# Side work of an attention, expert and feed-forward kernel put in other places

## The chip, the cores and the metric

The kernel runs on one core of one Trainium2 chip. The core has a matrix engine (TensorE, PE in the profile, with its weight loads as PEld), a vector engine (VectorE, DVE), a scalar engine (ScalarE, ACT), GpSimd (POOL) and a sequencer that only issues DMAs here (SyncE, SP). Each engine works through its own instructions in order and waits on semaphores for the others. The metric is the device time of one execution in microseconds (us), less is better, given as the median of the runs.

## The reference

```python
def reference(**kwargs):
    attn_out = _attn_ref(q, k, v, cap)          # (4, 12, 448, 64)
    x = attn_out.transpose(0, 2, 1, 3).reshape(1792, 768)
    x = _moe_ref(x, ...)                        # 8 experts, 768 -> 1024 -> 768
    return _moe2_ref(x, ...)                    # 768 -> 1536 -> 768

def _attn_ref(q, k, v, cap):
    scores = cap * np.tanh(q @ k.T / 8 / cap)
    attn = np.exp(scores - scores.max(-1)); attn /= attn.sum(-1) + 1e-09
    return attn @ v

def _moe_ref(x, modality_id, w_gate, modality_bias, w1, w2):
    logits = x @ w_gate + modality_bias[modality_id]
    e_idx = np.argmax(logits, axis=1); gate_w = softmax(logits)[e_idx]
    for e in range(E):
        mask = e_idx == e
        out[mask] = gate_w[mask, None] * (np.maximum(x[mask] @ w1[e], 0.0) @ w2[e])

def _moe2_ref(x, w_gate, w_val, w_out):
    return (sigmoid(x @ w_gate) * (x @ w_val)) @ w_out
```

The output is float32 throughout.

## The kernel before, in words

All matrix products are made on PE in f16. A float32 operand is split in two f16 parts: "hi", the operand itself rounded, and "lo", the operand less hi. Nearly every split is one ACT instruction for hi and one DVE (or GpSimd) instruction for lo that reads what ACT wrote, so the two engines pass work back and forth.

The kernel is written under a manual schedule: the order in which the Python code issues instructions is the order on each engine, and nothing reorders them.

**Attention** goes over 4 batches and 12 heads; a step makes exponentials of scores on ACT (L300, L305), products on PE (L314, L316) and sums of exponentials on DVE (L325, L327, L333); L318 copies a finished head pair out of PSUM. The table `AFTER` (L66) lists for each batch after which step side work is issued. Its entry for the third batch holds the start of the experts: `w1` loads of the first expert's first weights, `w1s` their split (`split_w` L676: six pieces of 128x1024, hi L687, lo L689), `gather` the fetching of tokens into `xg` (L695, an indirect DMA that GpSimd issues), `trx` (L710) the transposes of those tokens on PE (L705) with their hi on ACT (L707) and lo on DVE (L708) into `xT`, and `w2` the loads of the second weights. `M["trs"]` lists the PSUM banks that transposes take in turn (L248); at this point it is one bank.

**Experts.** Tokens are sorted by expert into blocks of 128 rows; 15 blocks have work with this input, 14 of them always (`NFULL`). `step(s, fill)` (L764) is a block, run one behind: the products with w1 of block s (`mm1`, 36 matmuls of 512 columns), relu, w1's split for the next block if its expert is new, transposes of block s+2, then `fill[0]`, the DMAs that are due, the first half of block s-1's products with w2 (`mm2`, 24 matmuls of 384 columns), the transposes of block s's hidden values (`trh`), the second half, the output `put_y` (ACT L753, DVE L754, indirect DMA L755) and `fill[1]`. The fills hold work for the feed-forward: its weights arrive as 64-bit floats and are converted by three integer DVE operations and an ACT scale (`conv_ops` L836 to L847), two conversions a block; weight sums `wo_job`; and `y_sums` (L950).

**Feed-forward.** It uses Winograd's scheme with seven products and needs sums of blocks of its left operand. `y_sums(sup, p)` makes them for 128 rows p: four stages a, b, d, e, each of two or three DVE operations, a hi on ACT (L905) and a lo on DVE (L902); `y_more` (L1348) does the same under a condition on the number of blocks. The tokens go through in two groups (sup 0 with 512 columns, sup 1 with 384). In sup 1 the sums stand among weight sums (L883, L905, L910) and the copies and additions of sup 0's last products (ACT L1112, DVE L1115). `rest` (L1339) runs the blocks beyond 14 as they exist; behind it the passage (L1404 to L1420) begins the feed-forward's products (L1019) and does the last block's `mm2`.

Of the kernel before, what the change touches and what calls it, by code (L numbers as in the profile page):

```python
# [69 lines left out]
def tile_kernel(ctx: ExitStack, tc: tile.TileContext, q, k, v, cap, mod, wg, mb, w1, w2, gw, vw, ow, out, dbg=None):  # L70
# [1545 lines left out]
```

## Time and profile before

| | us |
|---|---|
| median of 3 runs (lowest, highest) | 1010.03 (1008.42, 1010.03) |
| the profiled execution's own time | 1006.74 |
| its span in the trace | 1004.8 |
| PE busy | 927.0 (92%) |
| DVE busy | 716.5 (71%) |
| ACT busy | 503.0 (50%) |
| GpSimd busy | 178.2 (18%) |

The profiled execution's mean granted TensorE clock is 0.978 of full. All rows are from that one execution. Attention lies at 0 to about 254 us, the experts at 254 to about 540, the feed-forward behind. In a row of a timeline the bracket tells how long the engine had been idle and which instruction released it; a letter q behind an engine's name is its sequencer (branches, register loads).

### The profile page before, as it was taken

Reading aid. Unit: us, or ns where it says so; the run is one execution under the profiler, and the core shown is the slowest. Engines: PE = TensorE matmul, PEld = TensorE weight load, DVE = VectorE, ACT = ScalarE, POOL = GpSimd, SP = SyncE. Lnnn points to the kernel's source line nnn. Section 1 sums busy time; section 2 is a strip of 40 time slices with the busy share of each in tenths; the row PEclk is TensorE's granted clock in tenths of the full one; section 3 lists DMA queues with packets and bytes.
Section 4 is the critical chain, followed back from the end, with each engine's and each line's share of the span. In section 5 each row is a group of like instructions: output and inputs, shape, how many; then the busy total and the mean of one; then the engine's idle time right before and its main releaser. Section 6 shows DMA issues by size and latency. Waiting matters only on the chain. (4 is left out here: it accounts for less than half of the span.)

```text
span 1004.8 us, 14723 instructions
## 1 busy us (share of the span) xinstructions
PE 927.0 (92%) x5291; PEld 474.4 (47%) x5291; DVE 716.5 (71%) x1239; ACT 503.0 (50%) x814; POOL 178.2 (18%) x219
## 2 busy tenths in 40 slices
PE   6998989876999899999996999999989899999997
PEld 2333333332455445555454444444556456666554
DVE  4879889689584896468773899997698754545651
ACT  5978769665414463334451665544344345554320
POOL 3000000001012131111120000000000078883131
PEclk9999999998899999999998999999999999999999
DMA  5534464446235678767930464321062132220001
GB/s 126 156 109 117 113 186 120 123 135 230 80 105 189 222 252 273 224 200 256 299 103 29 113 234 165 111 95 63 17 99 106 48 110 80 68 75 1 1 32 64
DMA packets 120491, 128.78 MB, mean 128 GB/s; under 512 B 75232, under 2 KB 100720, under 8 KB 119632
## 3 DMA queue, kind: packets, MB, share of 16 engines
q1 hardware_dynamic: 116288, 108.22, 35.6%
q0 software_dynamic: 4112, 19.46, 5.8%
q8 instruction: 44, 0.72, 0.3%
q14 instruction: 47, 0.39, 0.1%
HBM read 91.16 MB, written 30.99 MB: 122 GB/s over the span
## 5 line engine op out<-in xcount | busy, mean ns | idle before, releaser
L745 PE MATMUL sc<-w2s,hs 128*128 128x384 f16 x720 | 126.3, 331 | 13.3 <-ACTq L767 4.3
L1019 PEld LDWEIGHTS <-wa 128*128 128x128 f16 x909 | 89.8, 99 | 90.0 <-issue 11.6
L726 PE MATMUL sc<-w1s,xT 128*128 128x512 f16 x540 | 121.4, 383 | 0.9 <-DVE xT L708 0.7
L1019 PE MATMUL pp<-yr,wa 128*128 128x512 f16 (+1 forms) x468 | 101.7, 373 | 9.5 <-DVEq L1341 7.9
L745 PEld LDWEIGHTS <-hs 128*128 128x128 f16 x720 | 71.1, 99 | 57.9 <-issue 12.1
L300 ACT ACTIVATE E<-sc,sct 128x896 f32<-128x896 f32 x72 | 72.4, 1006 | 44.6 <-PE sc L292 43.5
L726 PEld LDWEIGHTS <-xT 128*128 128x128 f16 x540 | 53.2, 99 | 64.8 <-issue 3.2
L1019 PE MATMUL pp<-zr,wa 128*128 128x384 f16 x441 | 75.8, 326 | 0.6 <-ACT yr L1067 0.6
L305 ACT ACTIVATE E<-E,capt 128x896 f32<-128x896 f32 x72 | 74.7, 1038 | 0.6
L883 DVE TENSOR_TENSOR sta<-sta 128x384 f32<-128x384 f32 x108 | 71.0, 696 | 3.5 <-POOL y L910 2.5
L1019 PE MATMUL pp<-wos,yr 128*128 128x384 f16 x378 | 63.7, 331 | 8.0 <-ACT hs L1112 8.0
L314 PE MATMUL ot<-E,vf 128*64 128x448 f32 x288 | 70.4, 570 | 0.0
L1101 POOL DMA_INDIRECT out_dram<-hs,pm x14 | 14.0, 998 | 273.1 <-DVE hs L1115 198.9
L292 PE MATMUL sc<-qT,kT 64*128 64x448 f16 x432 | 56.2, 368 | 0.8 <-DVE kT L259 0.8
L1019 PEld LDWEIGHTS <-yr 128*128 128x128 f16 x378 | 37.5, 99 | 34.2 <-issue 10.6
L1019 PEld LDWEIGHTS <-wb 128*128 128x128 f16 x378 | 37.0, 98 | 34.5
L905 ACT ACTIVATE wa<-sta 128x384 f16<-128x384 f32 x98 | 48.6, 513 | 7.2 <-DVE sta L883 4.2
L1049 DVE TENSOR_TENSOR yr<-yr,pp 128x384 f32<-128x384 f32 x24 | 13.2, 552 | 43.1 <-PE pp L1019 43.1
L1019 PE MATMUL pp<-yr,wb 128*128 128x512 f16 x189 | 43.9, 379 | 0.0
L999 PE MATMUL pp<-wos,sta 128*128 128x384 f16 x252 | 41.9, 326 | 0.0
L708 DVE TENSOR_TENSOR xT<-tr,xT 128x384 f16<-128x384 f32 x34 | 17.4, 552 | 33.8 <-ACT xT L707 31.8
L910 POOL TENSOR_TENSOR wa<-sta,wa 128x384 f16<-128x384 f32 x42 | 40.1, 972 | 4.1 <-ACT wa L905 4.1
(308 smaller groups left out, 1598.6 us busy)
## 6 DMA issues: line engine op xcount, KB each, us to landing
sta<-g SPq DMA_DIRECT2D x40, 384.0 KB, 3.1
st<-in_moe_w_dram SPq DMA_DIRECT2D x8, 1536.0 KB, 10.2
sta<-in_moe_w_out_dram SPq DMA_DIRECT2D x12, 768.0 KB, 4.4
sta<-in_moe_w_val_dram SPq DMA_DIRECT2D x12, 768.0 KB, 6.3
g<-sta SPq DMA_DIRECT2D x18, 384.0 KB, 3.0
qf<-in_q_dram SPq DMA_DIRECT2D x48, 112.0 KB, 3.3
kf<-in_k_dram SPq DMA_DIRECT2D x48, 96.0 KB, 2.8
vf<-in_v_dram SPq DMA_DIRECT2D x24, 192.0 KB, 3.1
```

Source lines behind the costliest of these rows:

```text
L292: nc.tensor.matmul(sc[:, h, :S], kt_[p, a, 128 * j:128 * j + 128], qt_[p, b_], start=i == 0, stop=i == 2)
L300: nc.scalar.activation(out=e, in_=src, func=AF.Tanh, scale=sct)
L305: nc.scalar.activation(out=e, in_=e, func=AF.Exp, scale=capt)
L314: nc.tensor.matmul(ot[g][64 * h:64 * h + 64, :S], vf[g][:, h, j], e[:, h], start=j == 0, stop=False)
L708: nc.vector.tensor_tensor(out=lo, in0=pt[:, :128 * n], in1=hi, op=ALU.subtract)
L726: nc.tensor.matmul(p[:, nh], xT[s % 2][:, a, kk], w1s[:, b_, kk, 512 * nh:512 * nh + 512], start=i == 0, stop=i == 17)
L745: nc.tensor.matmul(M["p2"][:, nh, :384], hT[par][:, a, kk], w2s[:, b_, kk, 384 * nh:384 * nh + 384], start=i == 0, stop=i == 23)
L883: tt = lambda eng, o, x, y, op: eng.tensor_tensor(out=o, in0=x, in1=y, op=op)
L905: nc.scalar.activation(out=hi, in_=src, func=AF.Copy)
L910: los = [lambda x=x, d=d, e=e: e.tensor_tensor(out=d[1], in0=x, in1=d[0], op=ALU.subtract) for x, d, e in todo]
L999: nc.tensor.matmul(bk[p][:, c0:c1], l(p, a, kk), r(p, b_, kk)[:, c0:c1], start=i == 0, stop=i == 3 * kn - 1)
L1019: nc.tensor.matmul(bk[c][:, c0:c1], l(p, a, kk), r(p, b_, kk)[:, c0:c1], start=i == c0 == 0 and p in (1, 2, 7), stop=i == 3 * kn - 1 and c ...
```

## The change

It has four parts.

1. At attention's end the six hi pieces of the first weights go from DVE to GpSimd; their lo pieces get places of their own (`w1l`), the last two of them behind the first transposed block. The transposes there get two PSUM banks in turn instead of one. The last two quarter loads of w2 are issued a few steps later.
2. `step` has three fill lists, the new one between the block's transposes and the second half of `mm2`; a block's two conversions are spread over the three (three DVE operations; ACT scale and three DVE operations; ACT scale); due DMAs are issued at the block's end; `y_sums` of blocks 10, 12 and 13 go to the block's end.
3. In `y_sums` the lo of a stage is issued behind the next stage's DVE operations.
4. The last `y_sums` of sup 0 (p = 3), which stood in block 14 under a condition, is issued at the passage, behind the first 27 matmuls of the feed-forward.

```diff
 AFTER, entry of the third batch
-'w1s': (14, 15, 17, 17, 18, 19), 'idx': (11, 11), 'gather': (17, 18, 26), 'trx': (24, 26), 'w2': (20, 21, 22, 22)})
+'w1s': (14, 15, 16, 17, 18, 19), 'w1l': (16, 17, 18, 19, 25, 25), 'idx': (11, 11), 'gather': (17, 18, 26), 'trx': (24, 26), 'w2': (20, 21, 26, 26)})
 def step(s, fill=((), (), ()), more=None):
...
         for f in fill[0]:
             f()
-        while M["due"]:
-            M["due"].pop(0)()
         mm2(s - 1, (0,))
         trh(s)
+        for f in fill[1]:
+            f()
         mm2(s - 1, (1,))
...
-        for f in fill[1]:
+        for f in fill[2]:
             f()
+        while M["due"]:
+            M["due"].pop(0)()
 def y_sums
+        def lo_of(i, x, eng):
+            eng.tensor_tensor(out=l[x], in0=w[i], in1=h[x], op=ALU.subtract)
...
-            split(w[0], h[5], l[5], lo[0])
+            split_hi(w[0], h[5])
 
         def b():
             tt(w[1], h[3], w[0])
             nc.vector.tensor_tensor(out=w[1], in0=w[1], in1=l[3], op=ALU.add)
-            split(w[1], h[6], l[6], lo[1])
+            split_hi(w[1], h[6])
+            lo_of(0, 5, lo[0])
...
-            split(w[3], h[4], l[4], lo[3])
+            split_hi(w[3], h[4])
+            lo_of(2, 7, lo[2])
+            lo_of(3, 4, lo[3])
 attention, third batch
-                    add(n0 + o["w1s"][i], lambda i=i: split_w(st1, w1s, nc.vector, parts=(i,)))
...
+                add(n0 + o["trx"][0], M.update, {"trs": [3, 0]})
                 for s in range(2):
                     add(n0 + o["trx"][s], trx, s)
+                for i in range(6):
+                    add(n0 + o["w1s"][i], lambda i=i: split_w(st1, w1s, nc.gpsimd, None, parts=(i,)))
+                    add(n0 + o["w1l"][i], lambda i=i: split_w(st1, w1s, None, parts=(i,)))
 blocks
-                    step(s, ([lambda: y_more(3, fewv < 16)], []) if s == NFULL else ((), ()))
+                    step(s)
...
-        YS, YF = (10, 12, 13), (0, 0, 0)
+        YS, YF = (10, 12, 13), (2, 2, 2)
...
+        def conv_fill(fill, units):
+
+            c = [conv_ops(u[0], CV["raw"][e], CV["cvt"][e]) for e, u in enumerate(units)]
+            fill[0].extend(c[0][:3])
+            fill[1].extend((c[0][3],) + c[1][:3])
+            fill[2].append(c[1][3])
...
-                fill[0].extend(y_sums(0, 0))
+                fill[2].extend(y_sums(0, 0))
 passage
-        y_more(3, fewv > 15)
-        y_more(3, fewv < 15)
         g = {s: gset(0, s) for s in range(2)}
         for p in (1, 2, 7):
             g[0](p, 0, 256)
+        for f in y_sums(0, 3):
+            f()
```

Line numbers of the changed kernel are a few higher: L902 becomes L904 (L962 inside `y_sums`), L883 L885, L910 L912, L957 L959, L1115 L1124, L1341 L1353.

DVE at attention's end, from the last pieces of w1 to the two blocks' transposes. `w1s` are the split weights, `w2s` here the room of the sums of exponentials, `xT_119` and `xT_120` the first and second transposed block. Before:

```order
L687 TENSOR_SCALAR w1s<-st_113 128x1024
L689 SCALAR_TENSOR_TENSOR w1s<-st_113,w1s 128x1024
L333 TENSOR_TENSOR w2s<-w2s,EM 64x448 x2
L318 COPY OT<-ot 128x448
L325 TENSOR_TENSOR w2s<-E 128x896
L327 TENSOR_TENSOR w2s<-w2s,E 128x896
L333 TENSOR_TENSOR w2s<-w2s,EM 64x448 x2
L318 COPY OT<-ot 128x448
L708 TENSOR_TENSOR xT_119<-tr,xT_119 128x384 x2
L708 TENSOR_TENSOR xT_120<-tr,xT_120 128x384 x2
```

And with the change:

```order
L327 TENSOR_TENSOR w2s<-w2s,E 128x896
L689 SCALAR_TENSOR_TENSOR w1s<-st_113,w1s 128x1024 x3
L333 TENSOR_TENSOR w2s<-w2s,EM 64x448 x2
L318 COPY OT<-ot 128x448
L325 TENSOR_TENSOR w2s<-E 128x896
L327 TENSOR_TENSOR w2s<-w2s,E 128x896
L333 TENSOR_TENSOR w2s<-w2s,EM 64x448 x2
L318 COPY OT<-ot 128x448
L708 TENSOR_TENSOR xT_119<-tr,xT_119 128x384 x2
L689 SCALAR_TENSOR_TENSOR w1s<-st_113,w1s 128x1024 x2
L708 TENSOR_TENSOR xT_120<-tr,xT_120 128x384 x2
```

Before, four pairs L687, L689 stood behind the first L327 in a row (the last is shown); now three L689 stand there, no L687 is on DVE, and two L689 stand between the two blocks' lo.

GpSimd in the same place with the change; `xg` are the gathered tokens. Before, the rows are the same without those of L687.

```order
L687 TENSOR_SCALAR w1s<-st_113 128x1024 x3
L695 DMA xg_117<-xs,idxa 128x776
L687 TENSOR_SCALAR w1s<-st_113 128x1024
L695 DMA xg_118<-xs,idxa 128x776
L687 TENSOR_SCALAR w1s<-st_113 128x1024 x2
L711 COPY gt_123<-xg_117 128x1
```

Three hi pieces stand ahead of the first gather, one between the gathers, two behind them.

DVE in block 14, ahead of the passage; `hs` are the transposed hidden values, `y` the output of block 13. Before:

```order
L785 COPY ilast<-idxb 128x1
L1349 COMPARE_AND_BRANCH
L957 TENSOR_TENSOR sta<-yr 128x384 x2
L962 TENSOR_TENSOR sta<-sta 128x384
L902 TENSOR_TENSOR yr<-sta,yr 128x3x128
...
L977 TENSOR_TENSOR sta<-sta,yr 128x384
L902 TENSOR_TENSOR yr<-sta,yr 128x3x128
L1349 UNCONDITIONAL_BRANCH x2
L708 TENSOR_TENSOR hs<-tr,hs 128x512 x2
L754 SCALAR_TENSOR_TENSOR y<-sc,gt_124,y 128x768
L1341 COMPARE_AND_BRANCH
```

And with the change:

```order
L785 COPY ilast<-idxb 128x1
L708 TENSOR_TENSOR hs<-tr,hs 128x512 x2
L754 SCALAR_TENSOR_TENSOR y<-sc,gt_124,y 128x768
L1353 COMPARE_AND_BRANCH
```

The sums that stood between the block's index copy and its hidden values' lo are gone from the block.

DVE in sup 1's sums; `zr` holds the operand, `sta` the room for sums. Before:

```order
L957 TENSOR_TENSOR sta<-zr 128x384 x2
L962 TENSOR_TENSOR sta<-sta 128x384
L902 TENSOR_TENSOR zr<-sta,zr 128x3x128
L957 TENSOR_TENSOR sta<-zr,sta 128x384
L967 TENSOR_TENSOR sta<-sta,zr 128x384
L902 TENSOR_TENSOR zr<-sta,zr 128x3x128
L957 TENSOR_TENSOR sta<-sta,zr 128x384 x2
L902 TENSOR_TENSOR zr<-sta,zr 128x3x128
L1115 SCALAR_TENSOR_TENSOR hs<-pp,hs 128x384
```

And with the change:

```order
L959 TENSOR_TENSOR sta<-zr 128x384 x2
L967 TENSOR_TENSOR sta<-sta 128x384
L959 TENSOR_TENSOR sta<-zr,sta 128x384
L972 TENSOR_TENSOR sta<-sta,zr 128x384
L962 TENSOR_TENSOR zr<-sta,zr 128x3x128
L959 TENSOR_TENSOR sta<-sta,zr 128x384 x2
L962 TENSOR_TENSOR zr<-sta,zr 128x3x128
L1124 SCALAR_TENSOR_TENSOR hs<-pp,hs 128x384
```

Each lo (L902 before, L962 now) stands behind the next stage's two operations instead of right behind its own.

## Rows read from the trace of the kernel before

**Rows 1.** The page, busy time, share of the span and instructions of each engine.

```profile
PE 927.0 (92%) x5291; PEld 474.4 (47%) x5291; DVE 716.5 (71%) x1239; ACT 503.0 (50%) x814; POOL 178.2 (18%) x219
```

**Rows 2.** Waits, 200 to 800 us: engine, tile, line, releaser; us, times, longest.

```profile
PE tr L705 <- DVE xT L708: 10.4, 3, 8.0
...
PE pp L1019 <- DVEq L1341: 7.9, 1, 7.9
...
PE sc L745 <- ACTq L767: 4.3, 2, 3.9
```

**Rows 3.** Timeline, 226 to 256 us: start, duration, engine, line, operation, idle before.

```profile
232.29 1.04 ACT L305 ACTIVATE E<-E,capt 128x896 f32<-128x896 f32 x1
...
232.91 1.65 POOL L695 DMA_INDIRECT xg<-xs,idxa  x1 [184.99 <-DVE OT L318]
...
242.21 1.25 DVE L333 TENSOR_TENSOR w2s<-w2s,EM 64x448 f32<-64x448 f32 x2
...
248.47 0.56 DVE L708 TENSOR_TENSOR xT<-tr,xT 128x384 f16<-128x384 f32 x1
...
249.09 0.90 PE L705 MATMUL tr<-id,xg 128*128 128x128 f32 x3 [8.03 <-DVE xT L708]
...
253.94 2.34 PE L726 MATMUL sc<-w1s,xT 128*128 128x512 f16 x5
```

**Rows 4.** DVE's groups by line and shape, 226 to 262 us: busy us, mean ns.

```profile
L689 DVE SCALAR_TENSOR_TENSOR w1s<-st,w1s 128x1024 f16<-128x1024 f32 x6 | 7.4, 1225 | 0.2
L687 DVE TENSOR_SCALAR w1s<-st 128x1024 f16<-128x1024 f32 x6 | 4.1, 685 | 0.0
```

**Rows 5.** GpSimd's groups by line and shape, whole span.

```profile
L910 POOL TENSOR_TENSOR wa<-sta,wa 128x384 f16<-128x384 f32 x42 | 40.1, 972 | 4.1 <-ACT wa L905 4.1
...
L157 POOL MEMSET scr<- 128x776 f32 x1 | 0.7, 738 | 0.0
masks.py:199 POOL TENSOR_SCALAR_AFFINE_SELECT id<-id 128x128 f32<-128x128 f32 x1 | 0.3, 291 | 0.1
```

**Rows 6.** DVE's groups by line and shape, 560 to 800 us.

```profile
L883 DVE TENSOR_TENSOR sta<-sta 128x384 f32<-128x384 f32 x44 | 22.6, 553 | 0.4
```

**Rows 7.** The same view, 800 to 920 us, where GpSimd does L910.

```profile
L883 DVE TENSOR_TENSOR sta<-sta 128x384 f32<-128x384 f32 x44 | 38.0, 905 | 2.9 <-POOL y L910 2.5
```

**Rows 8.** DMA issues: KB each, median us to landing.

```profile
st<-in_moe_w_dram SPq DMA_DIRECT2D x4, 768.0 KB, 4.6
```

**Rows 9.** Timeline of ACT, 266 to 285 us.

```profile
269.38 2.94 ACT L685 ACTIVATE w2s<-st 128x1024 f16<-128x1024 f32 x3
```

**Rows 10.** Timeline, 326 to 346 us.

```profile
334.23 1.29 DVE L708 TENSOR_TENSOR hs<-tr,hs 128x512 f16<-128x512 f32 x2 [1.39 <-ACT hs L707]
...
339.64 5.71 PE L745 MATMUL sc<-w2s,hs 128*128 128x384 f16 x24 [3.89 <-ACTq L767]
```

**Rows 11.** Windows: length, busy us (count) by engine, granted clock, DMA share, GB/s.

```profile
340.00:345.00 5.00, 5.00 (x23) 2.55 (x22) 4.13 (x8) 1.55 (x3) 0.60 (x2) 0.70 0.67 171
```

**Rows 12.** Timeline, 484 to 504 us.

```profile
503.07 0.48 PE L745 MATMUL sc<-w2s,hs 128*128 128x384 f16 x2 [2.51 <-DVE y L754]
```

**Rows 13.** Timeline, 524 to 546 us.

```profile
526.20 1.02 DVE L957 TENSOR_TENSOR sta<-yr 128x384 f32<-128x384 f16 x2
...
528.16 4.06 PE L745 MATMUL sc<-w2s,hs 128*128 128x384 f16 x24
...
535.85 0.90 ACT L753 ACTIVATE y<-sc,gt 128x768 f16<-128x768 f32 x1
536.78 1.02 DVE L754 SCALAR_TENSOR_TENSOR y<-sc,gt,y 128x768 f16<-128x768 f32 x1
...
540.10 5.20 PE L1019 MATMUL pp<-yr,wa 128*128 128x256 f16 x27 [7.87 <-DVEq L1341]
```

**Rows 14.** Waits of DVE, 737 to 805 us.

```profile
DVE zr L902 <- ACT zr L905: 7.2, 12, 0.6
```

**Rows 15.** Timeline, 760 to 800 us.

```profile
783.48 10.53 PE L1019 MATMUL pp<-wos,yr 128*128 128x384 f16 x54 [3.00 <-ACT hs L1112]
...
795.92 4.38 PE L1019 MATMUL pp<-wos,yr 128*128 128x384 f16 x26 [1.91 <-ACT hs L1112]
```

More of the change, by code (lines that the diff above doesn't have):

```diff
@@ L64 @@
 ZBT = (0, 0, 0, 1, 1, 2, 3, 5, 6)
-AFTER = ({'g0': 1, 'g1': 1, 's': 1, 'e1s': 4, 'e1g': 5, 'route': 6, 'route_b': 8, 'ga': 9, 'gb': 10, 'gc': 12, 'sc': (10, 12, 14, 16), 'e2': (7, 10, 12, 17, 21, 24), 'xw': (26, 27)}, {'g0': 1, 'g1': 1, 's': 1, 'e1s': 4, 'e1g': 5, 'route': 6, 'route_b': 10, 'ga': 9, 'gb': 10, 'gc': 12, 'sc': (10, 12, 14, 16), 'e2': (7, 10, 12, 17, 20, 23), 'xw': (26, 27)}, {'g0': 1, 'g1': 1, 's': 1, 'e1s': 5, 'e1g': 5, 'route': 6, 'route_b': 7, 'ga': 10, 'gb': 11, 'gc': 13, 'sc': (10, 11, 12, 13), 'e2': (6, 9, 10, 11, 12, 13), 'xw': (15, 15), 'ta': (9, 9), 'w1': (11, 11, 14, 12, 13, 13), 'w1s': (14, 15, 17, 17, 18, 19), 'idx': (11, 11), 'gather': (17, 18, 26), 'trx': (24, 26), 'w2': (20, 21, 22, 22)})
+AFTER = ({'g0': 1, 'g1': 1, 's': 1, 'e1s': 4, 'e1g': 5, 'route': 6, 'route_b': 8, 'ga': 9, 'gb': 10, 'gc': 12, 'sc': (10, 12, 14, 16), 'e2': (7, 10, 12, 17, 21, 24), 'xw': (26, 27)}, {'g0': 1, 'g1': 1, 's': 1, 'e1s': 4, 'e1g': 5, 'route': 6, 'route_b': 10, 'ga': 9, 'gb': 10, 'gc': 12, 'sc': (10, 12, 14, 16), 'e2': (7, 10, 12, 17, 20, 23), 'xw': (26, 27)}, {'g0': 1, 'g1': 1, 's': 1, 'e1s': 5, 'e1g': 5, 'route': 6, 'route_b': 7, 'ga': 10, 'gb': 11, 'gc': 13, 'sc': (10, 11, 12, 13), 'e2': (6, 9, 10, 11, 12, 13), 'xw': (15, 15), 'ta': (9, 9), 'w1': (11, 11, 14, 12, 13, 13), 'w1s': (14, 15, 16, 17, 18, 19), 'w1l': (16, 17, 18, 19, 25, 25), 'idx': (11, 11), 'gather': (17, 18, 26), 'trx': (24, 26), 'w2': (20, 21, 26, 26)})
 @with_exitstack
@@ L762, in if_new, with step @@
         return tc.If(reg(2, s, engines) > 0)
-    def step(s, fill=((), ()), more=None):
+    def step(s, fill=((), (), ()), more=None):
         if s > 2:
@@ L972, in d @@
             tt(w[2], w[2], l[1])
-            split(w[2], h[7], l[7], lo[2])
+            split_hi(w[2], h[7])
+            lo_of(1, 6, lo[1])
         def e():
@@ L1355, in y_rest @@
                 y_load(0, tiles)
+        def conv_fill(fill, units):
[3 more added lines that the diff above has]
+            fill[2].append(c[1][3])
         for s in range(2, NFULL):
-            fill = [], []
+            fill = [], [], []
             i = s - WFILL
             if 0 <= i < NWO:
-                fill[0].extend(lambda i=i, e=e: conv(2, 2 * i + e, CV["raw"][e], CV["cvt"][e]) for e in range(2))
+                conv_fill(fill, [(2, 2 * i + e) for e in range(2)])
                 M["due"].append(lambda i=i: wo_raw(i + 1) if i + 1 < NWO else set_raw(early_sets[0]))
-                fill[1].extend(wo_job(halves(*CV["cvt"]), Z["w"], wst[i]))
+                fill[2].extend(wo_job(halves(*CV["cvt"]), Z["w"], wst[i]))
             if 0 < i <= NWO:
@@ L1367, in tile_kernel @@
                 n = early_sets[s - FILL]
-                fill[0].extend(lambda n=n, e=e: set_conv(n, e) for e in range(2))
+                conv_fill(fill, [unit(n, e) for e in range(2)])
                 M["due"].append(lambda n=n: set_keep(n))
@@ L1372, in tile_kernel @@
                 if n == 0:
-                    fill[1].extend(set_job(0, (nc.vector,) * 7))
+                    fill[2].extend(set_job(0, (nc.vector,) * 7))
             t = {5: 0, 6: 1, 7: 2}.get(s)
@@ L1395, in tile_kernel @@
             if s == 13:
-                fill[1].append(lambda: y_more(1, fewv > 15))
+                fill[2].append(lambda: y_more(1, fewv > 15))
             step(s, fill, more if s == 2 else None)
```

## Prediction, made before the changed kernel ran

> **What bounds the kernel now.** The page comes first: PE is busy 927.0 us of 1004.8, 92% [rows 1], so no more than the 77.8 us in which it is idle can be won without touching its matmuls, and the change touches none. The next view is the list of waits of PE, which says where those 77.8 us lie and who ends them. The reader should see three of the places that the change edits in it [rows 2]: PE's transposes of the first tokens wait 10.4 us for DVE's lo, once for 8.0; its first feed-forward matmuls wait 7.9 us for DVE's sequencer; and a block's second products wait 3.9 of 4.3 us for ACT's. Then come the timelines around each place, which show who is late in front of PE. A gain counts in full where PE, after it, keeps its distance to everything behind; that holds as long as the loads that feed it are issued by engines that have moved forward too.
>
> **The change part by part.** All sums are made against the profiled execution's own 1006.74 us; it lies 3.29 below the median, and I put the 3.29 back at the end. A measurement of this kernel tells apart about 0.2%, here 2.0 us.
>
> *Attention's end (term A).* Before, DVE goes through four pairs of hi and lo up to 242.21, then through the last sums and copies for 6.26 us, and starts the first lo of the transposed tokens at 248.47 [rows 3]. Only then may PE transpose into the one bank again, at 249.09, and the ping-pong of PE, ACT and DVE over that bank goes on until the products start at 253.94, 5.47 after the first lo. With the change the hi pieces, 6 x 0.685 us [rows 4], are off DVE, and two of the lo pieces stand behind the first block. The three lo left are held by attention itself: the sum ahead of them needs the exponentials that end at 232.29 + 1.04 = 233.33 [rows 3]. From there the sum takes some 1.1 (an estimate from the 1.25 of the tail's pair [rows 3]), three lo take 3 x 1.225 = 3.7 [rows 4], so the last sums start near 238.1 and, 6.26 later, the first lo at 244.4. With two banks I count from there one lo, one transposition and one more hi and lo less in line: 2.2 instead of 5.47 (what remains in line is a second pair of hi and lo, 2 x 0.56, and a transposition, 0.90; the last pairs lie beside PE's 0.90 of transposing). Undisturbed, the products would start at 246.5, which is 7.4 sooner. The two lo that now stand behind the first block are 2.4 us and are needed by the last third of the first products, so they cost nothing as long as those 18 matmuls start first.
>
> What speaks against 7.4 is GpSimd. The trace of before shows no split on it. The nearest rows are a fill of 776 columns, 0.738, which for 1024 columns is 0.97 (it reads nothing), and a subtraction of two operands over 384 columns, 0.972, which is 2.59 for 1024 [rows 5]. The split reads one operand and writes one, as does the selection over 128 columns, 0.291, of which perhaps 0.1 is fixed: some 1.5 for 1024. I take 1.5 and keep 0.97 and 2.59. That time itself is off the path: three pieces come before the first gather, in time that DVE and GpSimd have, since the gather waits 185 us anyway [rows 3]. The other three run while DVE does sums and lo with two operands in SBUF, and there the two disturb each other: DVE's sums of 384 columns take 0.553 [rows 6], and 0.905 in the stretch where GpSimd does its own [rows 7]. So 0.972 us of GpSimd cost DVE 0.35, and a split of 1.5 costs it 0.54; if DVE stands for the whole of a split, it is 1.5. The Trainium skill ("SBUF — State Buffer", section "Who interferes with whom") has a rule against this change: DVE and GpSimd share one pair of ports, which one instruction holds to its end, and a DVE instruction with two SBUF inputs contends with a GpSimd instruction that reads SBUF. By that rule three splits cost DVE 3 x 1.5 = 4.5, and A would be 2.9; the rows agree in direction, not in size. Between 0.54 and 1.5 I take 1.1 a piece, 3.3 for three, because a piece that meets DVE's longer operations (1.225 to 1.25) can miss more than one. **A = 7.4 - 3.3 = 4.1**, bounds 7.4 (no hold) and 7.4 - 3 x 2.59 = -0.4.
>
> The later quarter loads of w2 take 4.6 us to land [rows 8] and would be issued near 248 to 251; ACT wants the last of them at 269.38, or some 4 sooner with the rest [rows 9]. Over 8 us of cover are left, so nothing. The second gather goes out one split later, 1.5 us, and its tokens are transposed behind the first block's: nothing.
>
> *Blocks (term B).* In block 4 the two conversions, six DVE operations, stand ahead of the hidden values' lo; DVE gets to it at 334.23, having waited 1.39 for ACT, which has scales of the conversions ahead of its hi [rows 10]. PE resumes at 339.64 after 3.89 for ACT's branch. With the scale of the second conversion behind the hi, the lo and everything up to the branch comes **1.3** sooner (the 1.39 less what the moved order costs). The granted clock of the matmuls behind that gap is 0.70 [rows 11], they take 5.71 for 24 against 4.06 elsewhere [rows 10, 13]; a gap of 2.6 may still end in a low clock, so I count nothing for it here. In the later blocks PE stands at most 2.51 us for DVE's output lo [rows 12], because `y_sums` stands ahead of that lo; behind it, the sums delay ACT's splits of the next weights, and raw loads that are now issued at a block's end come later. I put this at 0, with 2.5 us on either side: that wait goes, or one like it comes.
>
> *Passage (term C).* In block 14 the conditional sums start at 526.20 and hold up the hidden values' lo and the output lo at 536.78 [rows 13]. PE's second half of 24 matmuls, from 528.16, could have followed in 4.06 us: 532.22. Without the sums ACT's output takes 0.90 from there and DVE's lo 1.02, so it ends at 534.2; before it ended at 537.80, and PE started 2.30 behind it. 534.2 + 2.3 = 536.5 against 540.10: **C = 3.6**. The sums, moved behind the first 27 matmuls (5.20 us), run beside those and the last block's 48 (two times 4.06); DVE and ACT have nothing else there. They take 526.20 to 535.5, 9.3 us, and less with their lo interleaved, against 5.20 + 8.12 = 13.3 of cover. If that cover were short by all of the sums, C would be gone.
>
> *Sup 1's sums (term D).* DVE waits 12 times 0.6 us for ACT's hi, 7.2 in all [rows 14], because each lo stands right behind its hi. The copies of sup 0's results stand behind those hi on ACT, and PE waits for the copies: 3.00 at 783.48 and 1.91 at 795.92 [rows 15]. Four or five waits lie ahead of each. Ahead of the first, weight splits stand between the stages and take over some of the waits (a lo waits for its own hi, which now comes at the same distance): I count 1.0 of some 2.5. Ahead of the second there is nothing else, five waits, 2.9 in all: the 1.9 goes. **D = 2.9**, bounds 1.0 (only the first) and 6.6 (both gaps whole, and 54 matmuls at 4.06 / 24 each, 9.1, instead of 10.53).
>
> *Interleaved sums elsewhere* run beside PE-bound stretches; the cover is PE's 92%. Nothing.
>
> **Sum:** 4.1 + 1.3 + 3.6 + 2.9 = 11.9; 1006.74 - 11.9 = 994.8; with the 3.29, **998.1 us** for the median.
>
> **The rivals.**
> *GpSimd holds DVE for the whole of long splits (R1).* At 2.59 each A is -0.4 and the time 998.1 + 4.5 = 1002.6. For it: the 0.905 of rows 7, and that GpSimd's two-operand rate is the only one that the trace has at some length. Against: one operand, not two. The rule cited above is this mechanism, and by its full hold the time would be 999.3 at 1.5 a split.
> *No hold, and the clock stays up (R2).* A is 7.4 (3.3 more), the shorter gap in block 4 keeps the 24 matmuls at 4.06 (1.65 more) and the 54 at 9.1 (1.4 more): 998.1 - 6.35 = 991.7. For it: gaps of 1.91 are followed by 26 matmuls in 4.38, full speed, and one of 2.51 and one of 3.00 were not [rows 12, 15]. Against: two gaps would stay above 1.9.
> *Loads take the place (R3).* If w2's later quarters land after ACT wants them, A is used up and the blocks keep their distance to the loads: 998.1 + 4.1 = 1002.2, and with a wait of 2.5 in a block 1004.7. Against: 8 us of cover [rows 8, 9].
> *Slower (R4).* GpSimd's splits are so long that three of them, with DVE standing, use up all other gains. The point is 3 x t > 3.3 + 11.9 = 15.2, t = 5.1 us a split. At 6 us: 18.0 - 15.2 = 2.8 over 1010.0, 1012.8. For it: no row shows a type change on GpSimd. Against: twice the longest bound of rows 5.
> *Nothing measurable (R5).* The terms are paid back in later stretches that are bound by weight loads: within 2.0 of 1010.
>
> **How the numbers follow.** The sum with its bounds 0.50 (993 to 1003 on its own), R1 0.18, R2 0.15, R3 0.09, R5 0.04, R4 0.04. The range 990.0 to 1006.0 takes in the first four and leaves out R4, R5 and the tails. Faster by over 0.2%: 0.50 + 0.18 + 0.15 + 0.09 = 0.92; same 0.04; slower 0.04.
>
> **What would show it.** A: the products behind attention start near 250 instead of 253.94, GpSimd's L687 takes about 1.5, and DVE's sums beside it are longer than 1.1. B: the wait before 339.64 shrinks to some 2.6. C: the wait for DVE's sequencer shrinks from 7.87 to 4.3, and the sums lie beside PE's matmuls. D: DVE's waits for ACT in sup 1 fall below 2, the gap of 1.91 is gone and that of 3.00 near 2. The prediction is wrong if GpSimd's splits last over 3 us, if ACT's w2 split waits for a DMA behind attention, or if a block gets a new wait over 3 us for raw weights.

## The result and the profile after

| | before | changed |
|---|---|---|
| median us (lowest to highest) | 1009.22 (1008.22 to 1010.03), 4 runs | 992.21 (991.73 to 993.66), 4 runs |
| ratio, 95% interval | | 0.9844 [0.9829, 0.9859] |
| profiled execution, span | 1006.74, 1004.8 | 991.73, 989.7 |

The change gains 17.0 us in the medians and 15.0 between the two profiled executions. The forecast was 998.1, with 990 to 1006 around it.

The page of the changed kernel, busy time by engine, stands against [rows 1]:

```profile
PE 923.1 (93%) x5291; PEld 473.5 (48%) x5291; DVE 713.3 (72%) x1233; ACT 504.5 (51%) x814; POOL 194.5 (20%) x225
```

PE does the same 5291 matmuls in 3.9 us less: a part of the gain is clock, not waiting. DVE is hardly freed (3.2 us), GpSimd has 16.3 more. Next the waits of PE, 200 to 800 us (us in total, times, longest), to be laid beside [rows 2]:

```profile
PE sc L745 <- ACT w2s L685: 6.1, 1, 6.1
PE sc L745 <- ACTq L767: 5.3, 3, 2.4
PE tr L705 <- DVE xT L708: 5.2, 1, 5.2
PE pp L1028 <- ACT hs L1121: 4.6, 3, 2.0
...
PE pp L1028 <- DVEq L1353: 2.6, 1, 2.6
```

The waits that the prediction named shrank: 10.4 to 5.2, 7.9 to 2.6, 3.9 to 2.4 for the longest of ACT's branch. At the top stands a new one, 6.1 us for ACT's split of w2. Where the time went is read best by marking the start of the same PE work in both traces (mm1 of a block is L726) and comparing the stretches; the columns to the right are runs of the next section.

| stretch, us | before | changed | lo at once | old fills | sums earlier | best |
|---|---|---|---|---|---|---|
| DVE's L473 (near 205) to the first products | 48.89 | 44.42 | 44.37 | 43.56 | 44.37 | 41.46 |
| block 0 to 2 | 37.16 | 37.43 | 37.40 | 36.80 | 37.38 | 36.99 |
| block 2 to 5 | 58.86 | 55.76 | 55.75 | 58.70 | 55.73 | 55.74 |
| block 5 to 10 | 88.43 | 87.88 | 87.89 | 88.59 | 88.38 | 87.90 |
| block 10 to 14 | 76.34 | 79.10 | 83.16 | 72.60 | 73.45 | 69.48 |
| block 14 to the 27 first feed-forward matmuls | 25.37 | 21.91 | 26.05 | 19.91 | 21.91 | 19.90 |
| those to the next 36 (the last block's 48 between) | 13.29 | 11.21 | 12.87 | 12.61 | 12.87 | 12.87 |
| from there to the end | 451.4 | 446.4 | 451.3 | 446.2 | 447.4 | 447.5 |

The column "best" is the second version of "Put together". L473 starts 0.5 us later in the changed trace, so the first row shows 4.47 where the products' absolute start shows 3.93. All stretches gain but two: block 0 to 2 loses 0.3 and blocks 10 to 14 lose 2.8. The first row is a rough measure: six executions with the same code up to there (changed, lo at once, old fills, sums earlier, and two more of the next section) lie between 43.56 and 45.33.

**Attention's end.** Timeline of the changed kernel, 226 to 262 us, beside [rows 3]:

```profile
229.04 2.77 POOL L687 TENSOR_SCALAR w1s<-st 128x1024 f16<-128x1024 f32 x1 [4.78 <-DMA st<-in_moe_w_dram]
...
230.67 1.26 DVE L333 TENSOR_TENSOR w2s<-w2s,EM 64x448 f32<-64x448 f32 x2
...
235.76 4.48 DVE L689 SCALAR_TENSOR_TENSOR w1s<-st,w1s 128x1024 f16<-128x1024 f32 x3
235.83 2.79 POOL L687 TENSOR_SCALAR w1s<-st 128x1024 f16<-128x1024 f32 x1
...
240.16 2.09 DVE L333 TENSOR_TENSOR w2s<-w2s,EM 64x448 f32<-64x448 f32 x2
...
242.93 1.90 DVE L325 TENSOR_TENSOR w2s<-E 128x896 f32<-128x896 f32 x1
...
248.07 1.02 DVE L708 TENSOR_TENSOR xT<-tr,xT 128x384 f16<-128x384 f32 x2
...
250.01 6.17 PE L726 MATMUL sc<-w1s,xT 128*128 128x512 f16 x18
...
252.20 3.49 DVE L689 SCALAR_TENSOR_TENSOR w2s<-st,w2s 128x1024 f16<-128x1024 f32 x3
```

A split takes 2.79 us on GpSimd. DVE reaches the first lo only 0.40 sooner than before (248.47), but the products start 1.94 behind it instead of 5.47. The three L689 at 235.76, beside a split on GpSimd, take 4.48 instead of the 3.49 of the three at 252.20.

**Blocks 3 to 5, the passage and sup 1.** One row each from the timelines around 334, 532 and 773 us, the counterparts of [rows 10, 13, 15]:

```profile
334.53 4.06 PE L745 MATMUL sc<-w2s,hs 128*128 128x384 f16 x24 [2.44 <-ACTq L767]
```

```profile
520.61 4.06 PE L745 MATMUL sc<-w2s,hs 128*128 128x384 f16 x24 [1.84 <-ACTq L767]
...
530.55 1.02 DVE L754 SCALAR_TENSOR_TENSOR y<-sc,gt,y 128x768 f16<-128x768 f32 x1 [3.49 <-ACT y L753]
...
532.09 3.11 PE L1028 MATMUL pp<-yr,wa 128*128 128x256 f16 x27 [2.65 <-DVEq L1353]
```

```profile
773.55 20.78 PE L1028 MATMUL pp<-wos,yr 128*128 128x384 f16 x126 [1.53 <-ACT hs L1121]
```

At all three places the gap shrank and, in this execution, the matmuls behind it ran at the upper clock: 24 in 4.06 instead of 5.71, 27 in 3.11 instead of 5.20, and the 54 and 72 matmuls of sup 1 in one piece without the second gap, 20.78 instead of 10.53 and 11.86. The granted clock in these stretches is 1.00, the upper of the two levels (2.4 GHz); before it was 0.70 behind the gap in block 4 [rows 11]. Windows of the changed kernel, with the columns of that group:

```profile
334.00:339.00 5.00, 4.47 (x30) 2.96 (x30) 4.15 (x9) 2.06 (x4) 1.44 (x2) 1.00 0.65 185
532.00:537.00 5.00, 4.91 (x40) 3.86 (x41) 2.51 (x5) 0.53 (x1) 1.01 (x1) 1.00 0.23 86
773.00:784.00 11.00, 10.45 (x64) 6.21 (x64) 10.64 (x23) 4.03 (x9) 0.00 (x0) 1.00 0.05 18
```

The upper clock does not always come with the shorter gap. Ten kernels of this document have the gap of block 4 at 2.41 to 2.44 us: in eight executions the 24 matmuls took 4.06 us, in two 5.74, here the run with one bank (PE's timeline, 320 to 440 us):

```profile
338.69 5.74 PE L745 MATMUL sc<-w2s,hs 128*128 128x384 f16 x24 [2.43 <-ACTq L767]
```

The gap of 2.65 at the passage ended at either level too (last section). So the 1.65 us of clock in block 4 and the 2.1 behind the passage are partly luck of the profiled execution.

DVE's 12 waits of 0.6 in sup 1 [rows 14] are one of 0.2 (waits of DVE, 725 to 795 us):

```profile
DVE zr L962 <- ACT zr L907: 0.2, 1, 0.2
```

**The new wait.** Timeline of the changed kernel, 474 to 512 us, at the passage from block 12 to 13:

```profile
481.84 0.56 DVE L846 TENSOR_SCALAR sta<-sta 128x768 int32<-128x768 int32 x1 [4.25 <-DMA sta<-in_moe_w_val_dram]
...
488.55 0.84 ACT L849 ACTIVATE sta<-sta 128x768 f32<-128x768 f32 x1 [2.49 <-DVE sta L848]
...
497.20 5.80 ACT L685 ACTIVATE w2s<-st 128x1024 f16<-128x1024 f32 x6 [0.58 <-DMA g<-sta]
...
498.31 6.72 PE L745 MATMUL sc<-w2s,hs 128*128 128x384 f16 x23 [6.12 <-ACT w2s L685]
```

The raw weights arrive late (DVE waits 4.25). Block 12's row sums, now at the block's end, keep ACT to 496.6; only behind their last hi may it split w2 for block 12's new expert, and PE stands for 6.12. The 23 matmuls behind that wait take 6.72 instead of some 3.9 at the upper clock; before, the wait there was 2.51 [rows 12] and the first 23 took 6.14, a short second wait included.

### The profile page after: what moved, and what is told of

Its sections match the earlier page's. It is cut to its first block, busy times and chain, and to the rows that moved or that the text cites. A ratio compares the mean times of both kernels' runs of the same rounds, so it can differ in the third digit from the quotient of the medians.

```text
span 989.7 us, 14718 instructions
## 1 busy us (share of the span) xinstructions
PE 923.1 (93%) x5291; PEld 473.5 (48%) x5291; DVE 713.3 (72%) x1233; ACT 504.5 (51%) x814; POOL 194.5 (20%) x225
## 5 line engine op out<-in xcount | busy, mean ns | idle before, releaser
L726 PE MATMUL sc<-w1s,xT 128*128 128x512 f16 x540 | 121.6, 384 | 0.9 <-DVE xT L708 0.7
L1028 PE MATMUL pp<-yr,wa 128*128 128x512 f16 (+1 forms) x468 | 99.6, 367 | 4.2 <-DVEq L1353 2.6
L726 PEld LDWEIGHTS <-xT 128*128 128x128 f16 x540 | 53.2, 99 | 65.0 <-issue 3.5
L885 DVE TENSOR_TENSOR sta<-sta 128x384 f32<-128x384 f32 x108 | 68.8, 676 | 2.4 <-POOL y L912 1.2
L687 POOL TENSOR_SCALAR w1s<-st 128x1024 f16<-128x1024 f32 x6 | 16.7, 2791 | 176.6 <-DMA st<-in_moe_w_dram 176.5
L912 POOL TENSOR_TENSOR wa<-sta,wa 128x384 f16<-128x384 f32 x42 | 40.4, 978 | 4.8 <-ACT wa L907 4.8
```

The costliest lines, as they stand in the source:

```text
L687: hi.tensor_scalar(out=h_[:, w], in0=s_[:, w], scalar1=SW, scalar2=None, op0=ALU.mult)
L726: nc.tensor.matmul(p[:, nh], xT[s % 2][:, a, kk], w1s[:, b_, kk, 512 * nh:512 * nh + 512], start=i == 0, stop=i == 17)
L885: tt = lambda eng, o, x, y, op: eng.tensor_tensor(out=o, in0=x, in1=y, op=op)
L912: los = [lambda x=x, d=d, e=e: e.tensor_tensor(out=d[1], in0=x, in1=d[0], op=ALU.subtract) for x, d, e in todo]
L1028: nc.tensor.matmul(bk[c][:, c0:c1], l(p, a, kk), r(p, b_, kk)[:, c0:c1], start=i == c0 == 0 and p in (1, 2, 7), stop=i == 3 * kn - 1 and c ...
```

## The experiments

All ratios are to the kernel before, measured beside it; times are medians, to be compared with the changed kernel's 992.21, with a margin of about 1 us, since the medians of the kernel before lie between 1008.05 and 1009.22 from one set of runs to the next. The columns of the table above are from the single profiled execution of each.

**Hi of the first weights back on DVE.**

```diff
-lambda i=i: split_w(st1, w1s, nc.gpsimd, None, parts=(i,))
+lambda i=i: split_w(st1, w1s, nc.vector, None, parts=(i,))
```

> The changed kernel with the six hi pieces back on DVE, at the places where GpSimd had them; lo pieces, two banks and all else as changed. Theory: GpSimd's pieces buy nothing. In the changed kernel's trace a piece takes 2.79 us on GpSimd and lengthens one DVE operation with two SBUF operands by 0.84 to 0.87 (1.24 to 2.11, 1.09 to 1.95, 1.25 to 2.09, 1.09 to 1.90), and on DVE it takes 0.685. So 991 to 993 us, the same as changed (992.2), and the first products behind attention start within 1 us of 250.0. Rival: DVE's 4.1 us that were freed are what attention's end gained; then 995 to 997 and a start at 253 to 254.

Measured: 993.16 us, 0.9843 [0.9821, 0.9865]; 44.82 us from L473 to the products, against 44.42. The same as the changed kernel, within the noise. DVE's groups from 205 to 255 us say why; first the changed kernel (busy us, mean ns):

```profile
L689 DVE SCALAR_TENSOR_TENSOR w1s<-st,w1s 128x1024 f16<-128x1024 f32 x6 | 8.0, 1381 | 0.0
L333 DVE TENSOR_TENSOR w2s<-w2s,EM 64x448 f32<-64x448 f32 x10 | 7.9, 788 | 0.2
L325 DVE TENSOR_TENSOR w2s<-E 128x896 f32<-128x896 f32 x4 | 6.0, 1508 | 0.1
```

and this run:

```profile
L689 DVE SCALAR_TENSOR_TENSOR w1s<-st,w1s 128x1024 f16<-128x1024 f32 x6 | 7.2, 1217 | 0.0
L333 DVE TENSOR_TENSOR w2s<-w2s,EM 64x448 f32<-64x448 f32 x10 | 6.2, 617 | 0.2
L325 DVE TENSOR_TENSOR w2s<-E 128x896 f32<-128x896 f32 x4 | 4.4, 1092 | 0.1
...
L687 DVE TENSOR_SCALAR w1s<-st 128x1024 f16<-128x1024 f32 x6 | 4.1, 684 | 0.0
```

Beside GpSimd the same operations take 0.8 + 1.7 + 1.6 = 4.1 us more, as much as the six hi take on DVE. The move to GpSimd took nothing off DVE. Besides the three operations of the attention's end above, two earlier ones stood beside a split (timeline of the changed kernel, 204 to 228 us); unhindered, they take 1.25 and 1.09:

```profile
217.95 2.11 DVE L333 TENSOR_TENSOR w2s<-w2s,EM 64x448 f32<-64x448 f32 x2
...
221.53 1.95 DVE L325 TENSOR_TENSOR w2s<-E 128x896 f32<-128x896 f32 x1
```

**One bank.** `{"trs": [3, 0]}` back to `{"trs": [3]}` in the changed kernel.

> The changed kernel with one PSUM bank for the transposes at attention's end. Theory: the gain of 3.9 us there is the second bank's, since in the changed trace the first lo of the transposed tokens starts at 248.07, only 0.40 sooner than before, and the products 1.94 behind it instead of 5.47. So 3.5 us slower than changed: 995 to 997, with the ping-pong of three steps of 2.1 us back. Rival: the first lo comes sooner by what GpSimd took over, and the bank is worth under 1 us: 992 to 993.5.

Measured: 996.85 us, 0.9877 [0.9861, 0.9894]; L473 to the products 48.60 us. The bank is worth 4.2 us in the trace, nearly all that attention's end gained (4.47), and 4.6 in the medians.

**Two banks alone.** The kernel before with that one line added.

```diff
+                add(n0 + o["trx"][0], M.update, {"trs": [3, 0]})
                 for s in range(2):
                     add(n0 + o["trx"][s], trx, s)
```

> The kernel before with the two PSUM banks alone for the transposes at attention's end; hi and lo of the first weights stay on DVE at their old places. Theory: the second bank is what attention's end gained (4.2 us lost when it was taken away, counted from DVE's L473 to the first products: 48.60 against 44.42), so alone it brings the products 3.4 to 4.2 us sooner than before, about 45 us behind L473, and 1004 to 1005. Rival: the two lo pieces moved behind the first block are needed too, as the bank only helps if DVE reaches the first lo when the transposes are done; then under 1 us.

Measured: 1004.28 us against 1009.19, 0.9953 [0.9941, 0.9966]; L473 to the products 45.61. One line gains 4.9 us in the medians, 3.3 in the stretch. PE's timeline of this run, 236 to 256 us, beside [rows 3]:

```profile
245.18 0.58 PE L705 MATMUL tr<-id,xg 128*128 128x128 f32 x3 [3.11 <-DVE OT L318]
...
250.10 1.54 PE L705 MATMUL tr<-id,xg 128*128 128x128 f32 x6 [4.34 <-DVE xT L708]
...
251.44 4.92 PE L726 MATMUL sc<-w1s,xT 128*128 128x512 f16 x12
```

The second transposition no longer waits for the first one's lo, and one step of the ping-pong is left instead of three. The rest of part 1 adds 1.2 at most (45.61 to 44.42), less than the row's own spread.

**Hi on DVE and ACT.** Pieces 0 to 2 on DVE, 3 to 5 on ACT behind the last exponential, their lo behind the first block.

```diff
-'w1s': (14, 15, 16, 17, 18, 19), 'w1l': (16, 17, 18, 19, 25, 25)
+'w1s': (14, 15, 16, 22, 22, 22), 'w1l': (16, 17, 18, 25, 25, 25)
...
-split_w(st1, w1s, nc.gpsimd, None, parts=(i,))
+split_w(st1, w1s, nc.vector if i < 3 else nc.scalar, None, parts=(i,))
```

> The changed kernel with nothing on GpSimd: hi of pieces 0 to 2 on DVE, of pieces 3 to 5 on ACT behind attention's last exponential (ACT is idle there, 240.7 to 243.0 and again to 249.6 in the changed trace), lo of pieces 3 to 5 behind the first transposed block. Theory: attention's tail is set by DVE; it loses six operations of 0.69 or holds of 0.86 less three, and one lo of 1.2: the products start 3.5 to 5 us sooner than 250.0, and the time is 987 to 989. Rival: the tail is set by PE and ACT (last exponential at 240.7 in the changed trace) and the three lo behind the block hold up the first products: 990 to 993.

Measured: 989.95 us, 0.9819 [0.9793, 0.9846]; L473 to the products 41.36, 3.1 less than changed, where 3.5 to 5 were expected. The time lies between the two expectations, at the rival's edge, and the interval overlaps with the changed kernel's; the stretch is clearer than the median, for the two later runs with these places took 40.48 and 41.46. In ACT's idle time three hi pieces held up nothing that the rows show; GpSimd's took back what they gave.

**Lo right behind its hi again.** `split_hi` and `lo_of` in `y_sums` back to `split`, all else as changed.

> The changed kernel with each lo of the row sums right behind its hi again. Theory: in the second group's sums the gaps of PE of 3.00 and 1.91 come back with the lower clock behind the first, 5.0 us, and in the blocks the sums behind the output take 2 us longer and hold up ACT's split of w2 in block 13 by as much: 998 to 1000. Rival: the sums' places matter and not their inner order (the second group gains by what comes before): 992 to 994.

Measured: 1007.57 us, 0.9989 [0.9970, 1.0007]. Outside both expectations: without this one part, 15.4 of the 17.0 us are gone, given the other parts. The table's column shows four places instead of two: blocks 10 to 14 4.1, the passage 4.1, the 27 matmuls behind it 1.7, sup 1 4.9. The 1.7 is clock behind a gap of nearly the same length (2.72) and can't be put down to this part. PE's waits in this run, 200 to 800 us, and its rows in the blocks and in sup 1:

```profile
PE sc L745 <- ACTq L767: 9.4, 3, 4.2
PE pp L1024 <- ACT hs L1117: 8.2, 4, 3.3
PE sc L745 <- ACT w2s L685: 7.1, 1, 7.1
```

```profile
458.20 5.52 PE L745 MATMUL sc<-w2s,hs 128*128 128x384 f16 x24 [2.72 <-ACTq L767]
...
525.78 5.74 PE L745 MATMUL sc<-w2s,hs 128*128 128x384 f16 x24 [4.22 <-ACTq L767]
```

```profile
781.94 10.61 PE L1024 MATMUL pp<-wos,yr 128*128 128x384 f16 x54 [3.28 <-ACT hs L1117]
794.38 11.86 PE L1024 MATMUL pp<-wos,yr 128*128 128x384 f16 x72 [1.82 <-ACT hs L1117]
```

Sup 1 is as it was before, gaps and clock. In the blocks the sums stand at the end of 10, 12 and 13, straight ahead of ACT's next split or branch. PE's waits behind them are 2.72, 7.1 and 4.22, where the changed kernel has 1.06, 6.12 and 1.84, and behind the first and the last the clock falls as well (5.52 and 5.74 for 24 matmuls instead of 4.06). Without interleaving, the new places are worse than the old ones: blocks 10 to 14 take 83.16 against 76.34 before.

**Interleaved sums alone**, in the kernel before.

> The kernel before with the interleaved row sums alone (part 3 of the change). Theory: undoing this part in the changed kernel cost 15.4 us (1007.6 against 992.2), in sup 1's sums 4.9, in blocks 10 to 13 4.1, in block 14 and behind it 5.8. Alone it gains the 5 us of sup 1, 3 to 4 in blocks 10 to 13 and 2 to 3 in block 14, where four waits of 0.6 go out of the gap of 7.9: 10 to 12 us, 997 to 999. Rival: it gains in the blocks only where the sums stand behind the output lo; then sup 1's 5 us are left, 1003 to 1004.

Measured: 997.74 us against 1008.47, 0.9891 [0.9875, 0.9908], a gain of 10.7: within 10 to 12. By stretches 3.6 in blocks 10 to 14, 2.6 in block 14, and 3.3 in sup 1, where 5 were expected: the gap of 1.91 is gone and that of 3.00 is 2.06, but the matmuls behind it kept the lower clock. Added to the two banks alone (4.9) it makes 15.6, nearly the whole change; the two together, without the rest, weren't run.

**Last sums in block 14 again**, under their condition.

```diff
-                    step(s)
+                    step(s, ([lambda: y_more(3, fewv < 16)], [], []) if s == NFULL else ((), (), ()))
```

and the unconditional ones behind the 27 matmuls taken out, the conditional ones of before put back ahead of them.

> The changed kernel with the last row sums of the first group in block 14 again, under the condition, interleaved as changed. Theory: PE's gap at the passage grows from 2.65 by what the interleaved sums take (7.5 us, less the 4 us in which PE does 24 matmuls), to 5 to 6.5, and the 27 matmuls behind it fall to the lower clock (5.2 instead of 3.1): 3 + 2 = 5 us slower, 996 to 998. Rival: only the wait counts, and the clock falls in the changed kernel too: 994.5 to 995.5. Third: the sums at the passage delay the feed-forward's first results by as much as they gave: 992 to 993.

Measured: 994.97 us, 0.9863 [0.9846, 0.9879], 2.8 slower in the medians, under the 5 that the theory gave and inside the rival's 994.5 to 995.5. In the trace block 14 is 3.0 longer (24.93) and the 27 matmuls and 48 behind them 1.4 (12.60). The 1.4 is clock, and six kernels without these sums in block 14 lost as much there, so only the wait is this place's: about 3 once the sums are interleaved.

**Old fills.** Both conversions, the due DMAs and the row sums of blocks 10, 12 and 13 ahead of the second products as before; sums interleaved.

```diff
         for f in fill[0]:
             f()
+        while M["due"]:
+            M["due"].pop(0)()
         mm2(s - 1, (0,))
...
-            fill[0].extend(c[0][:3])
-            fill[1].extend((c[0][3],) + c[1][:3])
-            fill[2].append(c[1][3])
+            fill[0].extend(c[0] + c[1])
...
-        YS, YF = (10, 12, 13), (2, 2, 2)
+        YS, YF = (10, 12, 13), (0, 0, 0)
...
-                fill[2].extend(y_sums(0, 0))
+                fill[0].extend(y_sums(0, 0))
```

> The changed kernel with the blocks' fills as before: both conversions and the row sums of blocks 10, 12 and 13 ahead of the second products, the due DMAs there too; the sums interleaved, attention's end and the passage as changed. Theory: the fills gained 3.1 us in block 4 (gap 3.89 to 2.44 and the clock kept) and lost 3.8 in block 13 (a wait of 6.1 for ACT's split of w2, behind raw weights that landed 4 us later and the sums); the two cancel: 991 to 993. Rival: the spread conversions gain in every block, the loss has another cause: 995 to 997. Third: the old places with interleaved sums gain what the new ones do: 988 to 990.

Measured: 987.75 us, 0.9809 [0.9787, 0.9830]: nearest to the third expectation, faster than the changed kernel by 4.5. Part 2 of the change costs on the whole. It gains 2.9 in blocks 2 to 5 and loses 6.5 in blocks 10 to 14 and 2.0 in block 14. PE's waits in this run (200 to 800 us) have ACT's branch at 3.9 again and no wait for ACT's split above 0.5:

```profile
PE sc L745 <- ACTq L767: 4.3, 2, 3.9
...
PE sc L745 <- ACT w2s L685: 1.9, 5, 0.5
```

**Raw weights asked for first.** The order of `set_keep` and `set_raw` among the due DMAs exchanged.

> The changed kernel with the next raw weights asked for ahead of the DMA that stores the converted ones, which waits for the second ACT scale at the block's end. Theory: raw weights of block 12 are asked for 1 to 1.5 us sooner (475.2 to 474), land as much sooner, and the wait of 6.1 us in block 13 becomes 4.5 to 5: 990.5 to 991.5. Rival: they land when the expert's own weights let them (both are in flight at 478 to 482), so nothing: 992 to 993.

Measured: 991.70 us, 0.9841 [0.9820, 0.9862]; by the median the two expectations can't be told apart. In the trace blocks 10 to 14 take 77.88 instead of 79.10 and the wait for ACT's split is 5.2 instead of 6.1: the late raw weights are a small part of it.

**Sums earlier.** `YS = (8, 10, 13)` instead of `(10, 12, 13)` in the changed kernel.

> The changed kernel with the first two row sums at the end of blocks 8 and 10 instead of 10 and 12. Theory: the wait of 6.1 us in block 13 is ACT's split of w2 standing behind the sums of block 12 (490.2 to 497.2); without them the split starts some 6 us sooner, at ACT's last scale (489.4), and the wait falls under 1: 5 to 6 us faster, 986 to 988. Rival: the raw weights that land late are the cause (both conversions of block 12 wait, 4.3 and 0.4 us) and leave 3 us of the wait, or blocks 8 and 10 have no room for the sums: 989 to 992.

Measured: 987.69 us, 0.9810 [0.9782, 0.9837]. Timeline of this run, 478 to 506 us:

```profile
483.17 0.56 DVE L846 TENSOR_SCALAR sta<-sta 128x768 int32<-128x768 int32 x1 [6.60 <-DMA sta<-in_moe_w_val_dram]
...
489.40 0.84 ACT L849 ACTIVATE sta<-sta 128x768 f32<-128x768 f32 x1 [2.02 <-DVE sta L848]
...
490.36 6.04 ACT L685 ACTIVATE w2s<-st 128x1024 f16<-128x1024 f32 x6
...
491.46 0.48 PE L745 MATMUL sc<-w2s,hs 128*128 128x384 f16 x2 [0.40 <-ACT w2s L685]
```

The raw weights are even later (6.60), yet the split follows the last scale at once and PE waits 0.40. So the sums' place at the end of block 12 is the cause of the new wait, shown by moving sums alone.

**Put together.** Hi on DVE and ACT; conversions spread over the fills in blocks 3 to 5 only (due DMAs at the end only there); from block 6 on conversions, due DMAs and sums ahead of the second products. The second version has its first two sums in blocks 8 and 10.

```diff
         for f in fill[0]:
             f()
+        while M["due"] and not fill[1]:
+            M["due"].pop(0)()
         mm2(s - 1, (0,))
...
-                conv_fill(fill, [unit(n, e) for e in range(2)])
+                fill[0].extend(lambda n=n, e=e: set_conv(n, e) for e in range(2))
...
-        YS, YF = (10, 12, 13), (2, 2, 2)
+        YS, YF = (8, 10, 13), (0, 0, 0)
...
-                fill[2].extend(y_sums(0, 0))
+                fill[0].extend(y_sums(0, 0))
```

> Three findings put together: hi of the first weights on DVE and ACT instead of GpSimd (as in the run with hi on ACT); conversions spread over the fills in blocks 3 to 5 alone; from block 6 on both conversions, the due DMAs and the row sums ahead of the second products, as before the change, with interleaved sums. Theory: the run with the old fills took 36.7 us less 19.9 from block 10 to the passage's 27 matmuls by the same blocks (72.6 + 19.9 against 79.1 + 21.9 changed, 8.5 us better) and lost 3.0 in block 4; attention's end gains another 3.1 counted from DVE's L473: 992.2 - 8.5 - 3.1 = 980.6; 979 to 983. Rival: what blocks 3 to 5 gain is waited for in block 6, where the raw weights of the first set are then late: 983 to 986.

> The same with the first two row sums in blocks 8 and 10 instead of 10 and 12. Theory: blocks 12 and 13 have new experts, whose w2 ACT splits behind the sums' hi (18.2 and 20.2 us with old fills against 17.1 of a block bound by PE); blocks 8 and 10 have room: 1 to 2 us faster than the other mixed version. Rival: blocks 8 and 10 have conversions and sums of the next set too and become longer than 17.1 by as much: the same within 1 us.

Measured: 980.20 us, 0.9726 [0.9710, 0.9743], and 978.01 us, 0.9703 [0.9684, 0.9722]. The first lies within the theory's 979 to 983. Both beat both kernels; the second is 14.2 us faster than the changed one and 2.2 faster than the first, where 1 to 2 were expected (their intervals overlap a little). Its blocks 10 to 14 take 69.48 against 72.30 in the first, near the 4 x 17.10 = 68.4 that a block bound by PE takes. PE's largest waits in it (200 to 800 us):

```profile
PE pp L1030 <- ACT hs L1123: 4.3, 3, 2.0
PE tr L705 <- DVE xT L708: 2.8, 1, 2.8
PE sc L745 <- DVE w2s L689: 2.7, 2, 1.9
```

## Why the prediction was right, and where its sum was off

The direction, the four places and the range held; the gain was put at 11.9 against the profiled execution and was 15.0. Term by term:

- **Term A, 4.1: right in size, wrong inside.** The stretch gained 4.5. The step that failed is the price of a split, "some 1.5", "2.59" at most: it took 2.79, over the upper bound. What it costs DVE was put at 1.1 a piece for the three late ones; they lengthened one operation each by 0.99, 0.84 and 0.81, while two of the three early ones, which the text put in time that GpSimd and DVE have, cost 0.86 each. Together that is about the 4.1 that the six hi gave back, so "undisturbed ... 7.4" was never there to be had from GpSimd. The gain came from "with two banks ... 2.2 instead of 5.47" (measured 1.94), as two runs show.
- **The rule on shared ports** (the Trainium skill, "SBUF — State Buffer", section "Who interferes with whom"). The trace fits it in that all five lengthened DVE operations have two SBUF inputs; none with one input began within the first 1.0 us of a split, so that these go free isn't shown. It does not agree that the pair is held for the whole instruction: the hold was 0.81 to 0.99 us in a split of 2.79, and L333 at 230.67 ran at its own 0.63 an operation while the split begun at 229.04 went on. Here the measurement decides. R1, built on the full hold, fell.
- **Term B, 1.3: mis-sized by the clock.** The gap went from 3.89 to 2.44, 1.45, as the moved order gave. The 24 matmuls behind it took 1.65 less, for which the text said "I count nothing for it here", since such a gap "may still end in a low clock". It did so in two of ten kernels, so the caution was sound and the 1.65 is not to be counted on. 1.45 + 1.65 is the 3.10 of the table.
- **The later blocks, "0, with 2.5 us on either side": the sum held, the price of a wait failed.** Blocks 5 to 10 gained 0.55 and 10 to 14 lost 2.76, 2.2 together and inside the 2.5. The sign of what the text foresaw, sums that "delay ACT's splits of the next weights", was the one that decided, and one such wait was 6.1 long with the lower clock behind it, not 2.5. Interleaving alone gained 3.6 here, and with the old fills 3.7: the new places gave back 6.5.
- **Term C, 3.6: 3.5 of wait and 2.1 of clock.** The gap shrank by 5.2, to 2.65 instead of the 4.3 of the forecast: PE followed DVE's output lo by 0.52 us, not by the 2.30 that was carried over from before. Block 14 gave 1.8 back in a wait that stands ahead of it (ACT's branch behind block 13's sums, 1.84 at 520.61). The 3.5 is therefore right partly by luck, and the 2.1 of clock is missing in six executions with the same gap.
- **Term D, 2.9: 5.0.** The first gap came out at 1.53 where 2 was expected, the second is gone, and the matmuls behind the first run at the upper clock, 1.6 more. The upper bound of 6.6 is added up wrongly, for 3.00 + 1.91 + 1.4 make 6.3; it held all the same. With the same interleaved sums, the stretch to the end took 444.9 to 448.1 us in eleven kernels, so the gain here is 3.3 to 6.4.
- **"Interleaved sums elsewhere ... Nothing" failed.** PE's 92% was no cover. In the kernel before, interleaving alone gained 3.6 in blocks 10 to 14 and 2.6 in block 14, 10.7 in all, where the prediction gave it the 2.9 of term D; without it, the changed kernel's places would have cost 4.1 and 4.1 more.

The clock in B, C and D is 1.65 + 2.1 + 1.6 = 5.4 us, more than the 3.1 by which the whole sum was off. R2 had two of these three, and its 991.7 is the nearest of the forecast's times, though its other half, no hold, did not come. The rest cancels: the 2.2 lost in the later blocks against small gains elsewhere. So the place of the result in the range owes something to luck: clock that was not counted stands against a wait that was not priced. Of the signs of being wrong, GpSimd's splits stayed under 3 us, and a block did get a new wait over 3 us, behind sums and not for raw weights.

## What to carry to other kernels

When two engines pass one item back and forth, put the second engine's step of an item behind the first engine's step of the next: a few lines of that alone gained 10.7 us here, and one more PSUM bank alone 4.9. Before work is moved to the end of a stage, look at what the next stage's first instruction on the same engine is and who waits for it; the sums at the end of block 12 made PE wait for 6.1 us, and 0.4 once they stood at the ends of blocks 8 and 10. A gap that shrinks may give back time in the matmuls behind it as well, so price a gap with the clock that the rows show behind it, and as a range: one execution does not tell which level comes.

## What the hardware showed

- A type change of 128x1024 from SBUF to SBUF took 2.79 us on GpSimd (2.76 to 2.86), 0.685 on DVE and 0.98 on ACT (2.94 for three). On GpSimd five of six lengthened one DVE operation with two SBUF inputs, by 0.81 to 0.99, that ran at the beginning of the split; later in the split DVE ran at its own speed.
- A gap of PE of the same length may or may not cost clock. Behind 2.65 us of waiting the 27 matmuls took 3.11 in the changed kernel and in the runs with hi on DVE and hi on ACT, but 4.51 to 4.78 in six others with 2.64 or 2.65, here in the run with sums earlier (PE's timeline, 500 to 545 us). The granted clock of this stretch is 0.64, against 1.00 in the changed kernel:

```profile
525.24 4.78 PE L1028 MATMUL pp<-yr,wa 128*128 128x256 f16 x27 [2.64 <-DVEq L1353]
```

- With the sums in block 14, PE followed DVE's last output lo by 2.30 to 2.49 us in four kernels (before, the last sums in block 14 again, interleaved alone, two banks alone), without them by 0.52 to 0.60 in the ten others. Why isn't shown.
